# Block products in the first pass over d_ff for two more groups of tokens, and four plain blocks for the last group's second pass

## The chip, the cores and the metric

The kernel runs on one core of one Trainium2 chip. The metric is the device time of one execution in microseconds; the time before is the median of three runs, 629.42 us (628.07 to 630.46). The engines are PE (TensorE), ACT (ScalarE), DVE (VectorE), POOL (GpSimd) and SP (SyncE, whose queue issues all DMAs here); PEld is PE's weight load, which overlaps its matmuls.

## The reference, cut to what matters

An attention with two sets of keys per query, and a feed-forward layer with softplus on its result:

```python
# q, k, v: (4, 8, 768, 64), float32; block 32, window 16
k_sum = k.reshape(B, H, 24, 32, D).max(axis=3)         # one key per block of 32
v_sum = v.reshape(B, H, 24, 32, D).mean(axis=3)
scores_l = scale * q @ k^T, kept where |i - j| < 16, else -1e9
scores_s = scale * q @ k_sum^T + log(32)
a = softmax over (768 local, 24 block) scores
x = (a @ [v, v_sum]) as (3072, 512)                     # tokens x d_model
h = x @ w_in                                            # w_in: (512, 2048), float64
g = max(h, 0) + log1p(exp(-|h|))                        # softplus
out = g @ w_out                                         # w_out: (2048, 512), float64
```

## The kernel before, in words

**Tiling.** The 3072 tokens are 12 chunks of 256, taken two at a time as six groups (`groups[x]`, x = 0 to 5, 512 tokens each). d_ff is 16 columns of 128 (`f` = 0 to 15). Both weight matrices do not fit at once, so there are two passes: groups 0 to 4 do columns 0 to 7, group 5 does all 16 (the second half of the weights arrives meanwhile, `arrive`), and then groups 4 down to 0 do columns 8 to 15. This is `phases`. The sums of a first pass are kept in HBM (`partial`) and added at the end of the second; the attention result of groups 0 to 4 is kept there too (`keep`) and loaded again for the second pass (`attended`).

**Precision.** Each float32 operand of the feed-forward layer is split in two fp32r parts: a rounding (`high`) and a remainder (`low`). A product is three matmuls (`TERMS`: high x high, high x low, low x high). Weights are turned from float64 bit patterns to such parts on DVE, ACT and POOL (`weights`).

**Attention** of a group runs in four units (`attention`, two chunks x two pairs of head pairs): scores on PE, a mask on DVE, exp on ACT, a normalisation, a transpose of 32 x 32 blocks on DVE, a store to HBM (`squares`) and four loads back (`pT`), then the product with the values on PE (`values`, result `xo`). The units of group x + 1 run beside the feed-forward layer of group x.

**Hidden columns, plain** (`hidden`). In the first pass, and for both halves of group 5, a column is 4 slices of d_model x 3 terms = 12 matmuls of 128 x 128 by 512 tokens into one PSUM bank `ph`. Its operand is `whole_x`, split by `prepare_whole`, or for group 5 straight from the bank.

**Hidden columns, by block products** (`hidden_pair`). In the second pass of groups 0 to 4, two columns are made together as a 2 x 2 by 2 x 2 block product with seven block products in place of eight: the four blocks are two halves of d_model and two chunks of 256 tokens. The seven left operands are three weight blocks and four sums of weight blocks (`sums_of_weights`, buffers `s0` to `s3`, listed in `s_bufs`); the seven right operands (`operand(x, 0)` to `operand(x, 6)`) are the blocks r11, r21, r22 and differences of r11, r12, r21, r22, made by `prepare` in place, with `less` (a subtraction) and `split` (a rounding and a remainder). Each product is 2 slices x 3 terms = 6 matmuls of 256 tokens, into two PSUM banks `hx` and `hy`; a copy `p1` and seven DVE combinations put the products together.

**Buffers.** Operands lie in rings `x0` to `x2` (two buffers each) and `x3` to `x6` (one each); `whole_x` uses the same rings, `x3` to `x6` for even groups and `x1`, `x2` for odd ones. The banks `ph`, `hx`, `hy` and `xo` share one ring of two PSUM banks. `t` is a ring of two for temporaries and output blocks.

**After the hidden columns** (`feed_forward`): ACT computes softplus twice (`gh` rounded, then exact in the bank), DVE the remainder `gl`, and PE adds 12 matmuls (`po`, line 1162) per column into four PSUM banks of 128 tokens x 512.

**Order.** Every step is a task added to `Order`, with an engine (or alternatives, marked a, b, c). The list `SEQUENCE` gives the order in which all tasks are issued; each engine and SP's queue work through theirs in that order, and semaphores follow from the tiles. The list is the output of a planner that estimates times; it was written anew with the change.

Of the kernel before, what the change touches and what calls it, by code (L numbers as in the profile page):

```python
# [147 lines left out]
0 3 4 162 43 1 5 6 51 7 44 8 9 10 11 12 13 14 15 16 17 18 19 20 21 22 23 24 25 26 27 28 29 30 31 32 33 153 45 47 68  # L148
154a 158a 34 155 163a 64 46 52 156 53 55 164 2 157 165 167a 72 54 35 57 189 69 36 159 59 160a 161 49 73 48 37 86 313
61 166 56 74 171 87 190 38 39 168 75 58 40 191 88 41 60 104 62 100 76a 172a 50 152 321a 180 192 176a 77 79 66 316 65  # L150
173 174 63 67 169 42 78 108 71 175 80 170 70 177 314 315 185 194 101 109 89 312 193 110 122 123 81 324 208 198 181a
103 90b 124 107 105 343 111 82 195 84 344 182 209a 91 102 136 106 196a 112a 346 183 199 184 92 93 94 95 325 83 213
178a 197 85 342 113 125 326 372 345 96 186 210 211 114 179 351 212 138 115 116 98 117 99 97 376 126b 127 317 118 120
327 214 200a 129 128 215a 130 354 137 217 131 373 246 218 380 328 329 134 330 140 132 121 141 355 133 320 119 135 201
247 319 356 248 390 255 249 392 393 331 223a 357 187 389 334 332 318 374 322 333 391 202 204 250 256 257 188 262 203
139 258 323 216a 358 259 359 263 227 219a 377 264 251 269 270 252 205 146a 398a 271 384 360 378 265 206a 401 375 220
272 253 266 228a 335 347 350 232 353 221 254 260 402 336 273 381 361 420 229 423 421 143 276 362 363 348 230 364 419
385 403 277 349 422 283 352 338 261 222 379a 382 404 386 284 231 428 278 236 279 237 207a 280 405b 267 431 285 286 365
233 406 407 234 515 366 516 224 268 274 287 432 433 238a 368a 235 383a 290 387a 394 291 408 396 388 225 292 149a 434
239 240 520a 517 297 241 410 411 400 397 340 409 275 298 226 435a 436 242 523 299 293 395 281 399 693 542 243 294 282  # L160
412 437 524 541 546a 424 370 543 426 300 244a 438 288 341a 525 245 147a 440 289 301 429 427 441 295 339 413 439 549
430 296 425 526 567 417 369 527 303 568 569 305 570 528 550 304 529 442 697 518 415 522 309 443 416a 302 447a 371a
418a 571 445a 448 446 576a 519 551 521 530 142 533 552 306a 449 450 532 553 451 458 531 459 452 453 554 579 597 598
600 307 599 460 601 454 699 455 555 456 695 461 580 606a 465 466 581 694 467 462 534 609 711 698 714 556 310a 457 535a
558 713 544 582 144 696 468 719a 710 583a 584 463 610 559 469 611 537 612 464 705 470 548 700 557 712 547 613a 545 414
585 472 473 539 474 701 475 479 476 150a 480 481 471 722 560 148 741 145 743 614 482 572 483 477 742 486 723 740 586
587 588 574 724 487 578 702 478 484 744 577 488 489 561a 575 573 706 589 493 749a 703 494 485 538 615 495 725 496 490
707 752 590 591 595a 497 771 770 491 500 726 540a 501 616 492 602 565a 727 593 563 603 608 594 618 502 503 753 617 504
566a 604 605 619 775a 704a 607 498 499 508 505 772 620 151 728 311 337 754 778 621a 564 625 506 715 596a 729 755 623
624 626a 627 628 708 731 796 756b 629 757 797 732 630 507 636 631 716 798 948 717 637 643 709 638 644 801a 720 639 730  # L170
718 645 721 640 650 651 646 509 779 804 652 647 653 758 949 444 654 308 510a 952 733 657 734a 367 889 664 658 632 665
892 759 633 512 891 780 781 782 760 745 513 634 888 562 956 953 635 641 642 897a 783 957 747 890 762 751 805 659 648
666 761 750 748 746 738 660 950 667 784 900 806 661 763 668 736a 764a 536 919 920 785 649 671 678 672 768a 807 773 922
786 655 673 679 808a 788 809 927 787 766a 674 680 954 774 776 777 921 918 675 656 737 769a 810 662 681 960 789 511 799
901 902 803 811 800 814 682 790a 930 951 663 669 670 813 676 966 903 904b 812 802 792a 905 677 683 815 816 818 968 820
794a 739a 931 767a 821 795a 793a 819 822 906 592 965 958 969 967 893 735 684 898 686 961 899 791 823 932 933 896 895
514 934 907 824 685 974a 825 687a 831 908 909 935 826 817 832 833 690 834 977 996 827 838 978 835 839 894 910 688a 845
691 840 955 841 842 959a 828 999 997 979 846 998 995 936 911 962 1004 937 980 923 925 847 848 1007 981 1092 829 830
836 849 982 837 852 939 1091 940 1093 853 926 843 1008 1096 924 928 854 855 856 1099 963 929 938 983 912 916a 689 941
1009 622 984 964 859 860 970 975 942 944 985 861 1010 973 862 1011 844 972 850 866 914 867 987 1012 868 1116 971 863  # L180
986 873 976 1120 1117 874 1115 1100 1013 869 692 870 875 988 876 765 1014 1000 1003 913 1123 946a 989a 1101 993 1140
1016 945 851 1015 857 915a 1427 917a 1428 1561 877 1562 858 864 865 871 872 994 1102 991a 878 1017 1002 1103a 1005
1143 1001 992 947a 1104 1124 1006 881 1018 1148a 880 879 1563 1019a 990 1142 1105 1021a 1022a 1125 882a 1023a 1433
1139 1024 1141 1025 1026 1094 1027 1028 1151 1034 1029 1035 1095 1030 1041 1567 1042 883 1167 1036 1106 1107 1037 1043
1109 1038 1168 1020 1108 1048 1170 1097 1126 1127a 1044 1049 1098 1050 1051 885 1045 1110 1128 1031 1113 1111 1171
1169 886a 1118 1129 1052 1130 1152 1153 1112 1114 1131 1032 1122 1033 1055 1154 1056 1062 1057 943 1133 1119 1155 1058
1063 1039 1132 1040 1429a 1046 1176 1179 1156 887 1121 1064 1437 1059 1134 1047 1065 1157 1066 1180 1135 1181 1182
1183a 884 1137 1144 1150 1158 1160 1136 1146 1145 1149 1053 1069 1161 1159 1147 1070 1054 1060 1071 1072 1434 1138
1162 1184 1163 1073 1061 1185 1076 1165 1571 1077 1078 1166 1440 1441a 1067 1068 1079 1080 1172 1173 1186 1568a 1074
1075 1081 1085a 1187 1164 1174 1084 1083 1177 1188 1178 1175 1438 1088 1439a 1442 1189 1190 1193 1191 1194 1082 1192  # L190
1086a 1087 1195 1196 1197 1198 1204 1205 1206 1089 1199 1207 1253 1254 1208 1574 1211 1200 1212 1271 1272 1218 1219
1276 1201 1213 1273 1214 1289 1220 1221 1274 1255 1202 1215 1225 1203 1275 1277 1278 1226 1256 1257 1258 1222 1232
1262 1290 1227 1233 1291 1279a 1209 1228 1210 1259 1216 1260 1261 1308 1263a 1292 1264 1267 1346 1294 1234 1235 1229
# [40 lines left out]
def kernel(  # L234
# [639 lines left out]
    def weights(pair):  # L874
# [6 lines left out]
        for outer, which in tiles:  # L881
# [81 lines left out]
            )  # L963


    s_bufs = {}

    def sums_of_weights(f):

# [365 lines left out]
```

## Time and profile before

| | |
|---|---|
| median of three runs | 629.42 us (628.07 to 630.46) |
| the profiled execution | 630.05 us, its span 628.3 us |
| mean granted clock of TensorE | 0.983 |
| PE busy / PEld busy | 609.2 us (97%) / 508.9 us (81%) |
| DVE / ACT / POOL busy | 388.0 (62%) / 328.0 (52%) / 162.0 us (26%) |
| moved by DMA | 104.39 MB, 166 GB/s on average |
| plain hidden columns, `ph` L1045 | 672 matmuls of 512 tokens |
| block products, `hx` and `hy` L1085 | 840 matmuls of 256 tokens |
| projections, `po` L1162 | 1152 matmuls of 512 |

Rows of the profile name an engine, a line and a tile: "PE ph L1045" is the matmul of line 1045 that writes `ph`. In the chain of work that ended last, a row has the start, the length and the number of instructions merged. In a row of grouped instructions stand the count, the busy time, the mean length of one in ns, and the idle time in front of them with what ended it. In a table of stages, the columns are the stage, its length, the busy time of PE, PEld, DVE, ACT and POOL with their instructions, the granted clock, the DMA share, and GB/s.

### The profile page before, as it was taken

The numbers are of one execution on the slowest core, as the hardware profiler recorded it, in microseconds if no ns is written. First come the engines' busy times: TensorE is split into PE (matmuls) and PEld (weight loads), VectorE is DVE, ScalarE is ACT, GpSimd is POOL, SyncE is SP. The second block draws the span as 40 slices with busy tenths as digits, with TensorE's granted clock in tenths as the row PEclk, the third lists the DMA queues.
The fourth block names the chain that finished last, engine by engine and source line by source line (L and its number), as shares of the span: only waits on it lengthen the run. The fifth ranks groups of instructions, "written<-read, shape, count | busy, mean of one in ns | idle before, by whom it ended". The sixth has DMA issues, their size and how long they took to land.

```text
span 628.3 us, 12022 instructions
## 1 busy us (share of the span) xinstructions
PE 609.2 (97%) x4452; PEld 508.9 (81%) x4452; DVE 388.0 (62%) x998; ACT 328.0 (52%) x809; POOL 162.0 (26%) x145
## 2 busy tenths in 40 slices
PE   8769999999999999999999999999999999999997
PEld 7557777788888878877888888899889899898995
DVE  5887997764457454535427979764557557655442
ACT  2898895965766676456526677441323122222220
POOL 3325435132213043002003443490111403002000
PEclk9868999999999999999999999999999999999999
DMA  9998887989998887885634632103122050030301
GB/s 303 265 272 268 254 264 233 262 261 231 272 263 253 259 268 220 254 236 158 212 116 155 222 127 84 34 34 118 51 76 78 17 185 1 35 100 1 104 32 67
DMA packets 88955, 104.39 MB, mean 166 GB/s; under 512 B 27489, under 2 KB 67009, under 8 KB 88129
## 3 DMA queue, kind: packets, MB, share of 16 engines
q1 hardware_dynamic: 88896, 103.62, 54.5%
q8 instruction: 35, 0.57, 0.4%
q14 instruction: 24, 0.19, 0.1%
HBM read 73.92 MB, written 27.26 MB: 161 GB/s over the span
## 4 chain that ended last, share of the span: by engine, by line
PE 85%; DMA 8%; SPq 3%; ACT 1%; DVE 1%; issue 1%; DVEq 0%; POOL 0%; POOLq 0%; ACTq 0%
PE po L1162 40%; PE ph L1045 21%; PE hx L1085 9%; PE hy L1085 7%; PE xo L727 3%; PE sc L629 3%; DMA raw<-w_in_dram 2%; DMA k<-kT_dram 2%; DMA squares<-tb 2%; PE warm L1236 2%; DMA kf<-kT_dram 1%; DMA q<-qT_dram 1%; DMA v<-v_hp_dram 1%; SPq L708 1%; SPq L523 1%
## 5 line engine op out<-in xcount | busy, mean ns | idle before, releaser
L1162 PE MATMUL po<-w,gh 128*128 128x512 f32 x768 | 204.2, 394 | 0.0
L1162 PEld LDWEIGHTS po<-w,gh 128*128 128x128 f32 x768 | 141.4, 188 | 30.6 <-issue 0.6
L1045 PE MATMUL ph<-xw,w 128*128 128x512 f32 x672 | 163.9, 395 | 2.1 <-DVE gl L1155 2.0
L1045 PEld LDWEIGHTS ph<-xw,w 128*128 128x128 f32 x672 | 125.6, 188 | 32.5 <-DVE gl L1155 2.8
L1162 PE MATMUL po<-w,gl 128*128 128x512 f32 x384 | 116.6, 397 | 0.0
L1162 PEld LDWEIGHTS po<-w,gl 128*128 128x128 f32 x384 | 70.9, 188 | 15.9 <-issue 0.5
L650 ACT ACTIVATE sp<-sp,nm 128x120 f32<-128x120 f32 x192 | 73.1, 382 | 5.9 <-DVE nm L642 5.7
L1147 ACT ACTIVATE gh<-hx 128x512 fp32r<-128x512 f32 x20 | 12.0, 599 | 114.9 <-DVE hx L1095 114.9
L948 POOL TENSOR_TENSOR t<-t,raw 128x1024 int32<-128x1024 int32 (+1 forms) x20 | 42.4, 2122 | 98.8 <-DVE t L934 28.4
L1155 DVE TENSOR_TENSOR gl<-ph,gh 128x512 fp32r<-128x512 f32 x56 | 38.0, 684 | 40.8 <-ACT ph L1151 39.3
L1147 ACT ACTIVATE gh<-ph 128x512 fp32r<-128x512 f32 x56 | 33.5, 598 | 53.4 <-PE ph L1045 48.5
L789 POOL TENSOR_TENSOR x<-r,x 128x512 fp32r<-128x512 f32 x18 | 24.5, 1370 | 82.0 <-ACT x L782 32.2
L642 DVE CUSTOM_DVE_ANT_0 sp<-sc,added 128x120 f32<-128x120 f32 x192 | 40.8, 277 | 4.9 <-PE sc L629 3.9
L663 POOL TENSOR_TENSOR sp<-sp,ss 128x960 f32<-128x960 f32 x10 | 18.4, 1843 | 87.6 <-DVE ss L658 62.8
L650 ACT ACTIVATION_READ_ACCUMULATOR sp<-sp,nm 128x1 f32 x192 | 36.0, 187 | 0.0
L1085 PE MATMUL hx<-x,sw 128*128 128x256 f32 x240 | 35.4, 283 | 0.0
L1085 PE MATMUL hx<-x,w 128*128 128x256 f32 x240 | 35.1, 282 | 0.0
L1085 PEld LDWEIGHTS hx<-x,w 128*128 128x128 f32 x240 | 32.8, 189 | 1.9
L696 DVE STREAM_TRANSPOSE tb<-sp 128x1024 f32<-128x1024 f32 x20 | 24.8, 1242 | 15.2 <-POOL sp L663 7.9
L1085 PE MATMUL hy<-x,sw 128*128 128x256 f32 x240 | 33.2, 282 | 0.0
L1151 ACT ACTIVATE ph<-ph 128x512 f32<-128x512 f32 x56 | 32.8, 591 | 0.0
L1085 PEld LDWEIGHTS hx<-x,sw 128*128 128x128 f32 x240 | 31.7, 189 | 0.5
(108 smaller groups left out, 821.6 us busy)
## 6 DMA issues: line engine op xcount, KB each, us to landing
squares<-tb SPq DMA_DIRECT2D x20, 512.0 KB
pT<-squares SPq DMA_DIRECT2D x80, 128.0 KB
raw<-w_out_dram SPq DMA_DIRECT2D x16, 512.0 KB
kf<-kT_dram SPq DMA_DIRECT2D x16, 384.0 KB
raw<-w_in_dram SPq DMA_DIRECT2D x6, 1024.0 KB
q<-qT_dram SPq DMA_DIRECT2D x20, 256.0 KB
raw<-r SPq DMA_DIRECT2D x20, 256.0 KB
part<-ob SPq DMA_DIRECT2D x10, 512.0 KB
```

What stands on the lines that cost most here:

```text
L629: nc.tensor.matmul(unit(g * NU + h * NPAIR + i)[r * QW:(r + 1) * QW, k0:k1], lhsT=q[rows, w * QW:(w + 1) * QW], rhs=k[rows], start=True, s ...
L642: nc.vector.tensor_tensor_reduce(out=sp()[:, n], in0=unit(n), in1=added()[:, kinds.index((lows[w], lows[w + 1]))], scale=-SCALE, scalar=FL ...
L650: nc.scalar.activation(sp()[:, n], sp()[:, n], AF.Exp, bias=nm()[:, n:n + 1], scale=-1.0, accum_out=ss()[:, n:n + 1],)
L696: nc.vector.transpose(out=tb().rearrange("p k (u q) -> p u k q", q=SQ), in_=tiles.sp().rearrange("p u (k q) -> p u k q", q=SQ),)
L789: engine.tensor_tensor(to(1), a(), to(0).bitcast(F32), op=ALU.subtract)
L948: nc.gpsimd.tensor_tensor(a, a, word(0, I32), op=ALU.add)
L1045: nc.tensor.matmul(ph(), lhsT=lhs(part, cc), rhs=xw[cc][0]()[:, xw[cc][1], a], start=cc == 0 and n == 0, stop=cc == NCC - 1 and n == 2,)
L1085: nc.tensor.matmul(to()[:, half], lhsT=lhs(wa, cc), rhs=of_x(xa)[:, cc * CH:(cc + 1) * CH], start=cc == 0 and m == 0, stop=cc == NG - 1 an ...
L1147: nc.scalar.activation(gh(), all_of(), AF.Softplus)
L1151: nc.scalar.activation(all_of(), all_of(), AF.Softplus)
L1155: nc.vector.tensor_sub(out=gl(), in0=all_of(), in1=gh().bitcast(F32))
L1162: nc.tensor.matmul(po[t](), lhsT=a()[:, t * P:(t + 1) * P], rhs=w2()[:, part, i2 * DM:(i2 + 1) * DM], start=f == f0 and i == 0, stop=f == ...
```

## The change

- Groups 4 and 5 (`SEVEN = 4` and above) make columns 0 to 7 by `hidden_pair` too. For that, the sums of the first half's weights are computed after the attention of group 4 is declared, and `attend` calls `prepare` in place of `prepare_whole` for them; group 5 takes its attention result to a block `r` first.
- Group 5's columns 8 to 15 are made by a new `hidden_blocks`: each chunk of 256 tokens by itself, from operands 0, 1 and 3 and the block r12, which is split for it into a third buffer of ring `x0`.
- The six loads of the first batch's v take the buffers of rings r0 to r2 in place of ring `gh`; keys and values of later batches would go to ring `t` if sums of weights existed by then.
- `SEQUENCE` is another list (2214 tasks, 2099 before). The computation of the attention is as before.

```diff
+    SEVEN = 4
 ...
-                part = buffer([P, DM], F32, "vn0", tag="gh", bufs=NU)
+                part = buffer([P, DM], F32, "vn0", tag=f"r{i // 2}", bufs=2)
 ...
-        if x and x < NX - 1:
+        if x and (x < NX - 1 or x >= SEVEN):
             r = block(2 * i + hp // NG)
 ...
             split(r11, *operand(x, 2), NG * CH)
+            if x == NX - 1:
+                held = single[x] = buffer([P, 2, NG, CH], F32R, "x", tag="x0", bufs=2)
+                split(r12, lambda part: held()[:, part].rearrange("p g c -> p (g c)"), (held,), NG * CH)
 ...
+    def hidden_blocks(x, f):
+        w, lhs = of_w(f)
+        ph = bank([P, CT], "ph")
+        x12 = single[x]
+        blocks = {(0, 0): operand(x, 0), (0, 1): operand(x, 1), (1, 1): operand(x, 3)}
+        blocks[1, 0] = (lambda part: x12()[:, part].rearrange("p g c -> p (g c)")), (x12,)
+        def product(i):
+            for hp in range(2):
+                of_x = blocks[i, hp][0]
+                for cc in range(NG):
+                    for n, (part, a) in enumerate(TERMS):
+                        nc.tensor.matmul(
+                            ph()[:, i * CH:(i + 1) * CH], lhsT=lhs(part, hp * NG + cc),
+                            rhs=of_x(a)[:, cc * CH:(cc + 1) * CH],
+                            start=hp == cc == n == 0, stop=hp == 1 and cc == NG - 1 and n == 2,
+                        )
+        for i in range(2):
+            task = order.add(PE, 1.43, lambda i=i: product(i), ..., [ph])
 ...
     def hidden(x, f):
+        if x >= SEVEN:
+            return hidden_blocks(x, f)
 ...
-        pairs = f0 > 0
+        plain = range(HALF, NF) if x == NX - 1 else range(HALF) if x < SEVEN else ()
         for f in range(f0, f1):
 ...
+            pairs = not (f0 <= f < f1 and f in plain)
 ...
                 if x < NX - 1:
                     keep(x, n, r[n])
+                if x >= SEVEN:
+                    prepare(x, n, r)
+                elif x < NX - 1:
                     prepare_whole(x, n, r)
 ...
             sums = attend(x, sums)
+            if x == SEVEN:
+                for f in range(0, HALF, 2):
+                    sums_of_weights(f)
```

More of the change, by code (lines that the diff above doesn't have):

```diff
@@ L153 @@
[L153 to L182, printed above, removed]
@@ new lines @@
+1568 1566 1472 1575 1460a 1571 1569 1573 1574 1576 1579 1577 1469a 1578 1678a 1519 1525 1572 1526 1580 1586 1587 1581
+1588 1591 1592 1593 1820 1532 1810 1473 1683 1594 1533 1534 1474a 1600 1536a 1535 1475a 1476a 1477a 1539 1537a 1597
+1582 1540a 1601 1583 1595 1602 1598 1596 1603 1604 1605 1599 1584 1606 1607 1585 1611 1612 1589 1813 1608 1613 1616
+1619 1618 1617 1620 1622 1621 1625 1689 1623 1624 1681a 1627 1590 1629 1626 1628 1630 1631 1636 1632 1609 1610 1637
+1684 1633 1614 1638 1685a 1641 1811a 1644 1642a 1692a 1645 1816 1647 1615 1541 1643 1693a 1646 1650 1648 1652 1694
@@ L230 @@
+2136 2072 2134 2132 2140 2076 2137 2119 2139 2135 2141 2142 2147 2143 2148 2120 2144 2149 2121 2125 2152 2155 2153a
+2126 2154 2156 2158 2159 2163 2157 2161 2165 2162 2166 2164 2167 2160 2168 2172 2169 2145 2146 2173 2174 2150 2177
+2180 2178a 2183 2179 2181 2184 2182 2186 2188 2151 2073 2187 2185 2189 2170 2192 2193 2171 2190 2194 2077 2191 2175
+2204 2209 2197 2176 2198 2199 2195 2196 2203 2202 2211 2200 2210 2213 2201 2205 2212 2206 2207 2208
 """
@@ L361, in declare @@
             for i in range(NHP):
-                kf = buffer([P, S], F32, "kf", tag=f"s{i % 2}", pool=wts, bufs=1)
-                st = buffer([P, n_t, P], F32, "st", tag=f"s{2 + i % 2}", pool=wts, bufs=1)
+                if s_bufs:
+                    kf = buffer([P, S], F32, "kf", "t", T_BUFS, dynamic=True)
+                    st = buffer([P, n_t, P], F32, "st", "t", T_BUFS, dynamic=True)
+                else:
+                    kf = buffer([P, S], F32, "kf", tag=f"s{i % 2}", pool=wts, bufs=1)
+                    st = buffer([P, n_t, P], F32, "st", tag=f"s{2 + i % 2}", pool=wts, bufs=1)
                 def load_k(i=i, kf=kf):
@@ L446, in keep_first @@
                 order.add(SP, 0.4, keep, [self.first_v], [(self.v, hp)], size=12 * KiB, row=512)
-    x_bufs = {}
+    x_bufs, s_bufs = {}, {}
     def x_of(x):
@@ L963, in weights @@
             )
-    s_bufs = {}
     def sums_of_weights(f):
-        order.group = f"s{f}"
+        order.group = f"s{f}" if f >= HALF else f"z{f}"
         a = buffer([P, 2, 2, CH], F32, "ws", "t", T_BUFS, dynamic=True)
@@ L975, in sums_of_weights @@
         begun = [order.writer[w, part] for w in held for part in range(2)]
-        if f == HALF - 2:
-            begun.append(products[-1])
         for k, w in enumerate(held):
@@ L1034, in of_w @@
         return w, lambda part, cc: w()[:, part, (cc * n + i) * P:(cc * n + i + 1) * P]
+    single = {}
+    def hidden_blocks(x, f):
[15 more added lines that the diff above has]
+        for i in range(2):
+            task = order.add(
+                PE, 1.43, lambda i=i: product(i),
+                [(*blocks[i, hp][1], part) for part in range(2) for hp in range(2)] + [(w, part) for part in range(2)],
+                [ph],
+            )
+            if not i:
+                first_after(task)
+        return [ph]
     def hidden(x, f):
+        if x >= SEVEN:
+            return hidden_blocks(x, f)
         w, lhs = of_w(f)
@@ L1140, in feed_forward, with all_of @@
             gl = buffer([P, CT], F32R, "gl", bufs=4)
-            def all_of(h=h):
+            def all_of(h=h, pairs=pairs):
                 return h().rearrange("p n c -> p (n c)") if pairs else h()
```

130 lines of the change are left out of this document (78 added, 52 removed).

## The prediction

> **What bounds the kernel now.** I read the page first, then a table of stages, the chain that ended last, and the waits.
>
> ```profile
> span 628.3 us, 12022 instructions
> PE 609.2 (97%) x4452; PEld 508.9 (81%) x4452; DVE 388.0 (62%) x998; ACT 328.0 (52%) x809; POOL 162.0 (26%) x145
> ```
> ```profile
> 0.00:51.90 51.90, 41.05 (x572) 32.85 (x572) 37.77 (x137) 35.67 (x123) 20.25 (x36) 0.80 1.00 285
> 51.90:110.00 58.10, 55.40 (x452) 42.75 (x449) 50.20 (x144) 47.89 (x121) 23.86 (x16) 1.00 0.84 249
> 110.00:322.00 212.00, 210.98 (x1699) 169.24 (x1699) 112.23 (x385) 134.73 (x389) 44.77 (x46) 1.00 0.81 237
> 322.00:412.00 90.00, 90.00 (x438) 74.24 (x439) 69.84 (x92) 55.74 (x77) 36.57 (x20) 1.00 0.35 120
> 412.00:628.30 216.30, 211.75 (x1303) 189.86 (x1301) 118.01 (x242) 53.98 (x102) 36.53 (x29) 1.00 0.19 65
> ```
>
> The stage rows give length, then busy time of PE, PEld, DVE, ACT and POOL, then granted clock, DMA share and GB/s. There are two regimes. Up to 51.9 us the DMA engines are full (share 1.00, 285 GB/s) and PE has holes; the granted clock is 0.80 there. From 110 us to the end PE is busy for 512.7 of 518.3 us, and 4.5 us of the rest are the last additions and stores, from 623.79 us on. A busy PE is modelled, so I check it with the chain, where a piece's length is the time really taken:
>
> ```profile
> 383.95 5.55 PE ph L1045 x24
> ...
> 594.40 1.43 PE hx L1085 x12
> 595.83 1.43 PE hy L1085 x12
> 597.25 1.43 PE hx L1085 x12
> 598.68 0.72 PE hy L1085 x6
> 599.40 4.61 PE po L1162 x20
> ...
> 623.79 0.69 DVE ob L1192
> ```
> ```profile
> PE xo L727 <- ACT pT L687: 4.2, 2, 2.4
> PE ph L1045 <- DVE gl L1155: 2.0, 2, 1.2
> ```
>
> The pieces follow each other without a gap, and the longest waits of PE (last two rows: total, times, longest) lie in the start. So after the start the time is the sum of what PE must issue, and a change of PE's work moves the end one for one, as long as the other engines keep up.
>
> **The change, part by part.**
>
> *Eight pairs of first-pass columns as block products.* Groups 4 and 5 each have 8 columns of d_ff in the first pass, 4 pairs each. A plain pair is 2 x 12 matmuls of 512 columns: the row at 383.95 has 24 of them in 5.55 us. A block pair is 7 products x 2 x 3 = 42 matmuls of 256 columns: the four rows from 594.40 have 42, and the next piece starts at 599.40, so 5.00 us. Saved: 8 x 0.55 = 4.4 us.
>
> *The last group's second pass from four plain blocks.* 24 matmuls of 256 columns (24/42 x 5.00 = 2.86 us) take the place of 12 of 512 (2.775 us): 8 x 0.08 = 0.66 us lost. PE's net is **-3.7 us**. Projections, scores and values are unchanged.
>
> The Trainium skill ("TensorE: Matmul & The Clock Gate", section "Wait — 56ns, not 53.3ns?") gives a back-to-back matmul as N / 2.4 GHz plus some 2.5 ns, an estimate of 216 and 109 ns; this trace has 5.55/24 = 231 and 5.00/42 = 119 ns. By the page the net would be -4.5 us; the rows decide, so -3.7 us.
>
> *What the block pairs ask of the other engines.* These rows price it:
>
> ```profile
> L1095 DVE TENSOR_TENSOR hx<-hx,u 128x256 f32<-128x256 f32 x20 | 8.6, 431 | 7.3 <-PE hx L1085 6.8
> L1104 ACT COPY p<-hx 128x256 f32<-128x256 f32 x8 | 3.0, 374 | 23.4 <-PE hx L1085 23.4
> L782 ACT CAST x<-r 128x512 fp32r<-128x512 f32 x21 | 12.8, 616 | 20.3 <-PE ph L1045 4.9 <-PE hy L1085 4.9 <-DMA r<-raw 4.8
> L789 DVE TENSOR_TENSOR x<-r,x x17: 676/682/1770, 267.4 to 567.7; 128x512 fp32r<-128x512 f32 x17
> L789 POOL TENSOR_TENSOR x<-r,x x18: 1285/1296/1832, 294.1 to 570.4; 128x512 fp32r<-128x512 f32 x18
> L797 DVE TENSOR_TENSOR r<-r 128x512 f32<-128x512 f32 x10 | 6.9, 687 | 1.4 <-POOL x L789 1.2
> L739 ACT COPY r<-xo 128x512 f32<-128x512 f32 x8 | 4.6, 580 | 7.5 <-PE xo L727 7.5
> L985 POOL TENSOR_TENSOR ws<-w 128x512 f32<-128x512 f32 x4 | 7.5, 1900 | 0.0
> L993 POOL TENSOR_TENSOR ws<-ws 128x256 f32<-128x256 f32 x1 | 0.7, 736 | 0.0
> L1016 POOL TENSOR_TENSOR sw<-ws,sw 128x1024 fp32r<-128x1024 f32 x2 | 4.8, 2394 | 1.2 <-ACT sw L1009 1.2
> 216.00:270.00 54.00, 54.00 (x452) 43.37 (x451) 28.16 (x107) 36.57 (x112) 13.36 (x14) 1.00 0.85 252
> 270.00:322.00 52.00, 50.98 (x358) 40.61 (x358) 22.93 (x69) 25.46 (x67) 6.34 (x5) 1.00 0.60 181
> 322.00:366.00 44.00, 44.00 (x218) 35.90 (x219) 31.62 (x45) 25.84 (x38) 13.94 (x9) 1.00 0.55 194
> 366.00:412.00 46.00, 46.00 (x221) 38.34 (x220) 38.22 (x48) 29.89 (x40) 22.64 (x11) 1.00 0.15 50
> ```
>
> Each pair adds 7 combinations on DVE (7 x 0.43 = 3.0 us) and a copy on ACT (0.37): 24 and 3 us over 8 pairs. Operands: each group now needs 7 splits of 512 columns (the last group one more, x12): a rounding (ACT 0.62) and a remainder (DVE 0.68 or POOL 1.30 at the median), and 4 subtractions (DVE 0.69), in place of 8 roundings and remainders of half the width; the last group also copies four banks (ACT 0.58). That is some 10 us more per group. The sums of the first half's weights, four times, are two or more POOL sums of 1.9 us, four small ones of 0.74, a rounding on ACT and a remainder (POOL 2.39). None of it is on PE. It lies beside group 4's first pass (270 to 322 us) and group 5's (322 to 366), where DVE is at 22.93 of 52 and 31.62 of 44 us. I went through the new order and added the row times of what each engine is given between the first product of a stage and that of the next: DVE has 41 us in the 53 us of PE's group 4 first pass, 36 in 42 in group 5's first pass, 31 in 40 in its second: 78, 86, 77%. The kernel before runs the 90 us from 322 with DVE at 69.84 (78%) and PE without a hole; 366 to 412 is at 83%. So throughput suffices; what can be lost is latency, at places where PE needs an operand just made. Two such places: group 3 to 4 (operands 1 and 2 lie in buffers that group 3's last plain product still reads) and 4 to 5 (operands 3 to 6, and x12, wait for group 4's last pair). In both the order leaves projections for PE between: 4.6 us per 20 (row at 599.40) against a copy, a subtraction, a rounding and a remainder, 0.6 + 0.69 + 0.62 + 1.30 = 3.2 us. Bounds: 0 when the cover holds, as between second-pass groups now, and 1.5 us at each place where it doesn't. I take +0.7 us in all. The one new wait, the rounding of x12 for the buffer of group 4's operand 0, has group 4's last softplus behind it on ACT; that softplus needs the sixth product of the pair, the rounding only the first, so it costs nothing.
>
> *Attention.* No unit is added or removed. Where `x >= SEVEN`, group 5 takes its bank into a block first. The values of a unit need a bank of the same ring of two that a pair takes whole.
>
> *The start, in a new order.* The six loads of the first v get six blocks of the r rings instead of four of gh, so this wait of the queue goes:
>
> ```profile
> SPq L423 <- PE vt L428: 1.8, 2, 1.0
> ```
> ```profile
> 104.66 3.66 DMA v<-v_hp_dram
> ```
>
> With the DMA engines full, what is late next is the bytes themselves. Task numbers below group 4 are the same in both lists, so I added the sizes that SP issues up to the last transfer that a step needs. Values of group 1: first unit 17.58 MB before, 18.68 after; second 21.61 and 22.13; third 25.64 in both; fourth 28.23 and 27.84. PE's last wait is the one before that fourth unit (the transfer at 104.66). At 249 GB/s, 0.39 MB is 1.6 us earlier; 1.1 MB in front of the first unit is up to 4.4 us later, if nothing fills PE. The first product of group 0 now stands in front of the last first-group transposes, which fills a hole. I take -0.5 us, nearest the fourth unit's row because that is where PE waits last, with -4 (the holes of the first 51.9 us: 10.9 us, of which a third might be filled) and +4.4 as ends. The wait of 1.8 us is in it.
>
> *Queues.* No transfer is added or dropped. The weights of the second half still land over those of the first once group 5 has passed them. The sums of the first half take the buffers where the last batch's keys and values were reduced, so they wait for attention of group 4, not the reverse; the branch for those keys in ring t is not reached, since no sum exists then. Cost nothing; if a sum is late, group 4's second product waits behind it on PE (bound: one sum, some 2 x 1.9 + 4 x 0.74 POOL and 2.4 us, 9 us, once).
>
> **Sum.** -3.7 (PE) +0.7 (latency) -0.5 (start) = -3.5 us. The profiled execution took 630.05 us (span 628.3), which would become 626.5; against the median of the runs, 629.42, it is **625.9 us**.
>
> **Rivals.**
>
> 1. *Latency eats the saving* (same). Eight pairs each losing 0.25 us plus 1.5 us at one handover: 3.5 us back, 629.4. For: DVE at 86% in group 5's first pass. Against: second-pass pairs lose nothing with the same seven combinations. A mechanism in the rows: the DVE remainder L789 is 0.68 at the median and 1.77 at most, and more POOL work lies beside DVE now. The Trainium skill ("GPSIMD Engine Reference", opening table, SBUF interfaces) says that GpSimd shares its SBUF interfaces with VectorE and contends with two-input instructions; that spread agrees.
>
> 2. *Attention late in group 4's first pass* (slower). The last unit takes this long now:
>
> ```profile
> 298.62 0.98 PE sc L629 x32
> ```
> ```profile
> 309.64 0.34 SPq L704 DMA_DIRECT2D squares<-tb  x1
> 321.87 1.15 PE L727 MATMUL xo<-pT,v 120*64 120x64 f32 x32
> ```
>
>    From scores to values 23.3 us, with DVE at 44%. The new order puts 23.0 us of PE work between the same two. If the mask, transpose and copy each queue behind a pair's combinations, a unit comes 2.5 us late, and PE, whose order is fixed, stops. Four units: +10 - 3.7 = +6.3, 635.7 us. It decides from (3.7 + 3.1)/4 = 1.7 us a unit. Against: the store starts 11 us after the scores, and its data had landed before PE came.
>
> 3. *The start goes better*: the holes fill by 3 to 4 us, 622.5. Against: the DMA share of 1.00.
>
> 4. *The start goes worse*: 1.1 MB in front of the first unit of group 1 is waited for in full: 629.42 - 3.7 + 0.7 + 4.4 = 630.8 (same).
>
> 5. *The change does not do what it says* would need 256-column matmuls to cost over 5.55/42 = 132 ns in the first pass; the second pass has them at 119. Under 1 in 50, inside rival 1.
>
> **How the numbers follow.** Forecast, 624 to 628: 0.50 (of it 0.38 below the bound). Rival 1: 0.20. Rival 2: 0.12. Rival 3: 0.12. Rival 4: 0.06. A change of under 0.5% (3.1 us) is what this measurement can hardly tell from none. Faster is below 626.3: 0.38 + 0.12 = 0.50; slower above 632.6: 0.12; same 0.38. The range 621.5 to 631.5 holds all but rival 2 and half of the fringes; the forecast's own is 624 to 628.
>
> **What would show it.** Right: 288 ph matmuls of 512 columns fewer, and 192 of 256 for group 5's second pass; hx and hy from 840 to 1176; PE without a wait from 110 us on, DVE near 80% between 270 and 400 us, the last attention unit on time. Wrong: PE waits for pT or for an x operand after 200 us; group 1 starting later than 110 us; a matmul of hx in the first pass longer than 119 ns.

## The result, and the profile after

The changed kernel takes 634.42 us (median of 4 runs, 633.86 to 636.03), the kernel before 629.41 us beside it (4 runs): ratio 1.0085, 95% interval [1.0058, 1.0112]. It is slower by some 5 us where 3.5 us less were forecast, and above the forecast range of 621.5 to 631.5 us. The profiled execution took 634.32 us; its page begins so:

```profile
span 632.5 us, 12633 instructions
PE 609.3 (96%) x4692; PEld 517.8 (82%) x4692; DVE 416.7 (66%) x1075; ACT 345.9 (55%) x842; POOL 191.1 (30%) x173
```

The table of stages of the changed kernel (length, busy time of PE, PEld, DVE, ACT and POOL, granted clock, DMA share, GB/s):

```profile
0.00:51.90 51.90, 40.70 (x541) 32.33 (x542) 32.61 (x125) 35.78 (x127) 19.47 (x35) 0.84 0.95 268
51.90:66.00 14.10, 10.90 (x96) 8.14 (x95) 13.16 (x34) 13.51 (x35) 3.85 (x3) 0.88 0.91 288
66.00:110.00 44.00, 41.35 (x338) 31.98 (x336) 42.24 (x104) 37.52 (x100) 17.80 (x10) 1.00 0.82 224
110.00:322.00 212.00, 211.34 (x1837) 172.29 (x1826) 135.56 (x443) 140.99 (x393) 70.72 (x73) 1.00 0.82 240
322.00:412.00 90.00, 89.97 (x575) 81.21 (x575) 72.87 (x125) 62.96 (x84) 38.56 (x24) 1.00 0.34 121
412.00:632.50 220.50, 215.02 (x1323) 191.88 (x1321) 120.27 (x248) 55.18 (x105) 40.73 (x30) 1.00 0.20 67
```

And the two stages of the kernel before that the prediction gave as one:

```profile
51.90:66.00 14.10, 13.24 (x58) 9.93 (x54) 12.19 (x31) 13.66 (x32) 6.88 (x5) 1.00 0.84 234
66.00:110.00 44.00, 42.15 (x395) 32.82 (x395) 38.00 (x114) 34.23 (x91) 16.98 (x12) 1.00 0.84 253
```

Between 51.9 and 66 us PE is 2.3 us less busy, at a granted clock of 0.88 in place of 1.00. (Over the whole execution the mean granted clock is 0.983 in both traces: in total the changed kernel is at half the clock no longer than the kernel before.) A busy time says too little here, since a matmul that waits or runs at half the clock counts as busy. So I laid each kernel's matmuls beside their order and gave each its length in an undisturbed stretch (0.231 us for 512 columns of ph, 0.230 of po, 0.119 for 256 columns, 0.031 a score, 0.034 a value). A time T minus the lengths of what PE has issued by T is the time that PE has lost by then (the warm-up is not counted as work). By these lengths all work together is 583.8 us before and 580.05 after: the block products do give 3.75 us. What PE had lost, in us:

| by the time (us) | 50 | 65 | 115 | 200 | 320 | 400 | 440 | end |
|---|---|---|---|---|---|---|---|---|
| before | 27.5 | 29.7 | 33.8 | 35.3 | 38.9 | 39.2 | 39.3 | 39.5 |
| changed | 28.0 | 34.0 | 38.9 | 42.2 | 44.7 | 45.7 | 48.0 | 48.3 |
| difference | 0.5 | 4.3 | 5.1 | 6.9 | 5.8 | 6.5 | 8.7 | 8.8 |

The difference of 8.8 less 3.75 is the 5 us of the medians (the two spans differ by 4.2: behind the last matmul 4.1 us are left, 4.9 before). 3.8 us of it come between 50 and 65 us, in group 0, and 2.2 between 400 and 440. Another 2.6 come between 65 and 200; of these 1.5 are listed waits of PE (3.2 us, most of them for `gl`, against 1.7), and the rest was not followed. From 200 to 320 us, which holds group 4's first pass, the changed kernel gains 1.1: the kernel before waits 1.0 us there, at 274.70, for ACT's `gh`.

**50 to 66 us.** PE in the kernel before, then in the changed one (start, length; idle time ahead and its releaser in brackets):

```profile
51.94 6.23 PE L1045 MATMUL ph<-xw,w 128*128 128x512 f32 x24
58.91 3.07 PE L1045 MATMUL ph<-xw,w 128*128 128x512 f32 x12 [0.74 <-DVE gl L1155]
```
```profile
54.08 1.15 PE L737 MATMUL xo<-pT,first 120*64 120x64 f32 x32
57.01 0.50 PE L1086 MATMUL ph<-xw,w 128*128 128x512 f32 x1 [1.78 <-ACT xw L767]
58.13 4.29 PE L1086 MATMUL ph<-xw,w 128*128 128x512 f32 x11 [0.62 <-DVE xw L771]
63.21 1.05 PE L639 MATMUL sc<-k,q 64*64 64x120 f32 x32 [0.80 <-ACT k L523]
```

Before, 24 products of columns 0 and 1 stand behind the last values of group 0, and the second operand is made under the first of them. In the new order 12 of them stand ahead of the values, so after the values nothing covers the 2.4 us in which ACT and DVE make the operand. The 11 matmuls after this hole take 4.29 us where 12 took 3.07, some 1.5 us more; with the 2.3 us that PE is less busy this makes the 3.8. Their clock:

```profile
58.00:61.40 3.40, 3.27 (x8) 2.60 (x9) 3.37 (x7) 3.38 (x15) 0.83 (x1) 0.50 1.03 326
```

So a hole of 2.4 us was followed by 3.4 us at half the clock. The Trainium skill ("TensorE: Matmul & The Clock Gate", section "Part 1: The HAM clock gate") has two clocks only, half and full, judged in windows of about 3.4 us; this row agrees in both numbers, though the hole was shorter than such a window.

ACT is what is late. Its rows in the changed kernel, then before:

```profile
55.55 1.15 ACT L935 ACTIVATE t<-raw 128x1024 f32<-128x1024 f32 x1
...
60.52 1.28 ACT L1189 ACT_TABLE_LOAD   x1
61.81 0.60 ACT L1189 ACTIVATE gh<-ph 128x512 fp32r<-128x512 f32 x1
...
63.06 2.23 ACT L953 ACTIVATE raw<-raw 128x1024 int32<-128x1024 uint32 x2
65.20 2.38 ACT L676 ACTIVATE sp<-sp,ss 128x120 f32<-128x120 f32 x8
67.49 0.57 ACT L1189 ACTIVATE gh<-ph 128x512 fp32r<-128x512 f32 x1
```
```profile
55.75 1.28 ACT L1147 ACT_TABLE_LOAD   x1
57.04 0.60 ACT L1147 ACTIVATE gh<-ph 128x512 fp32r<-128x512 f32 x1
...
59.61 0.57 ACT L1147 ACTIVATE gh<-ph 128x512 fp32r<-128x512 f32 x1
...
60.68 1.28 ACT L922 ACT_TABLE_LOAD   x1
...
63.16 1.28 ACT L1147 ACT_TABLE_LOAD   x1
...
67.08 1.28 ACT L922 ACT_TABLE_LOAD   x1
```

The softplus of column 1 (the second `gh` row) starts at 67.49 us, 17.2 us after the first product (50.30); before it was 7.7 us after it (59.61, 51.94). Ahead of it stand conversions of weights (L935, L953) and a normalisation (L676) that the order before did later or on another engine. Added up from the traces, ACT has worked 66.3 us by the start of that step in the changed kernel and 56.0 in the kernel before, 10.2 us more: 6.1 are two more normalisations, 3.1 conversions of weights. DVE has 57.3 against 55.7, 1.6 us more.

**425 us.** One wait of PE in the second pass, and behind it DVE and POOL of the changed kernel:

```profile
423.16 2.39 POOL L1025 TENSOR_TENSOR sw<-ws,sw 128x1024 fp32r<-128x1024 f32 x1 [6.29 <-DVE sw L1018]
...
425.59 0.69 DVE L1238 COPY ob<-po 128x512 f32<-128x512 f32 x1 [1.90 <-POOL sw L1025]
...
427.13 0.98 PE L1126 MATMUL hx<-x,sw 128*128 128x256 f32 x6 [1.73 <-DVE u L1136]
```

An output copy takes a buffer of ring `t` that a sum of weights still holds until POOL's remainder is made. DVE waits 1.90 us at the copy, the combinations of the next pair stand behind it, and PE waits 1.73 us for them. What such a hole costs is not always the same. The stretch behind it in the changed kernel, then in the profiled execution of run 11, which has the same wait of 1.73 us:

```profile
428.00:431.40 3.40, 3.40 (x19) 2.90 (x19) 2.15 (x5) 2.18 (x4) 0.00 (x0) 1.00 0.91 314
```
```profile
428.00:431.40 3.40, 3.40 (x15) 2.98 (x14) 2.16 (x6) 1.52 (x3) 0.00 (x0) 0.58 0.88 302
```

The granted clock stays at 1.00 in the one and is 0.58 in the other, where PE loses some 1.3 us more between 400 and 440 us.

**What was forecast of the blocks holds.** In the changed kernel, from the chain of waits, the groups of PE, and the stages of the prediction:

```profile
386.39 5.72 PE ph L1060 x48
```
```profile
L1086 PE MATMUL ph<-xw,w 128*128 128x512 f32 x384 | 97.2, 402 | 4.5 <-DVE gl L1197 2.1
...
L1060 PE MATMUL ph<-x,w 128*128 128x256 f32 x192 | 23.8, 282 | 0.0
```
```profile
270.00:322.00 52.00, 52.00 (x466) 45.40 (x465) 37.25 (x97) 33.14 (x83) 14.27 (x13) 1.00 0.58 178
322.00:366.00 44.00, 43.97 (x270) 38.99 (x270) 37.46 (x75) 27.74 (x40) 19.67 (x16) 1.00 0.55 193
366.00:412.00 46.00, 46.00 (x306) 42.22 (x305) 35.42 (x51) 35.22 (x45) 18.89 (x8) 1.00 0.14 51
```

288 plain matmuls fewer (672 to 384), 192 of 256 columns for group 5, 5.72/48 = 0.119 us each; DVE at 72, 85 and 77% of the three stages, and PE without a hole.

### The profile page after: what moved, and what is told of

Its sections match the earlier page's. It is cut to its first block, busy times and chain, and to the rows that moved or that the text cites. A ratio compares the mean times of both kernels' runs of the same rounds, so it can differ in the third digit from the quotient of the medians.

```text
span 632.5 us, 12633 instructions
## 1 busy us (share of the span) xinstructions
PE 609.3 (96%) x4692; PEld 517.8 (82%) x4692; DVE 416.7 (66%) x1075; ACT 345.9 (55%) x842; POOL 191.1 (30%) x173
## 3 DMA queue, kind: packets, MB, share of 16 engines
q1 hardware_dynamic: 88896, 103.62, 54.4%
## 4 chain that ended last, share of the span: by engine, by line
PE 81%; DVE 7%; DMA 5%; ACT 3%; SPq 2%; issue 1%; POOL 1%; ACTq 0%; DVEq 0%
PE po L1204 39%; PE hx L1126 12%; PE ph L1086 11%; PE hy L1126 9%; PE ph L1060 4%; PE xo L737 3%; PE sc L639 2%; DMA first<-v 1%; DMA kf<-kT_dram 1%; DMA raw<-w_in_dram 1%; ACT sp L676 1%; DMA k<-kT_dram 1%; DVE st L390 1%; DVE r L783 1%; DVE w L972 1%
## 5 line engine op out<-in xcount | busy, mean ns | idle before, releaser
L1086 PE MATMUL ph<-xw,w 128*128 128x512 f32 x384 | 97.2, 402 | 4.5 <-DVE gl L1197 2.1
L1086 PEld LDWEIGHTS ph<-xw,w 128*128 128x128 f32 x384 | 72.7, 192 | 22.3 <-DVE gl L1197 2.5
L799 POOL TENSOR_TENSOR x<-r,x 128x512 fp32r<-128x512 f32 x30 | 40.6, 1356 | 133.6 <-ACT x L792 77.0
L1126 PE MATMUL hx<-x,sw 128*128 128x256 f32 x336 | 49.2, 282 | 1.7 <-DVE u L1136 1.7
L1126 PE MATMUL hx<-x,w 128*128 128x256 f32 x336 | 49.3, 282 | 0.0
L1126 PEld LDWEIGHTS hx<-x,w 128*128 128x128 f32 x336 | 45.8, 189 | 3.7 <-DVE u L1136 0.3
L1126 PEld LDWEIGHTS hx<-x,sw 128*128 128x128 f32 x336 | 44.1, 188 | 2.7 <-DVE u L1136 2.2
L1126 PE MATMUL hy<-x,sw 128*128 128x256 f32 x336 | 45.6, 281 | 0.0
L1126 PEld LDWEIGHTS hy<-x,sw 128*128 128x128 f32 x336 | 42.7, 188 | 0.5
L1189 ACT ACTIVATE gh<-ph 128x512 fp32r<-128x512 f32 x40 | 23.9, 598 | 33.8 <-PE ph L1086 23.7
L792 ACT CAST x<-r 128x512 fp32r<-128x512 f32 x31 | 18.5, 617 | 26.2 <-POOL r L808 9.0
```

The costliest lines, as they stand in the source:

```text
L792: copy(out=to(0), in_=a())
L799: engine.tensor_tensor(to(1), a(), to(0).bitcast(F32), op=ALU.subtract)
L1086: nc.tensor.matmul(ph(), lhsT=lhs(part, cc), rhs=xw[cc][0]()[:, xw[cc][1], a], start=cc == 0 and n == 0, stop=cc == NCC - 1 and n == 2,)
L1126: nc.tensor.matmul(to()[:, half], lhsT=lhs(wa, cc), rhs=of_x(xa)[:, cc * CH:(cc + 1) * CH], start=cc == 0 and m == 0, stop=cc == NG - 1 an ...
L1189: nc.scalar.activation(gh(), all_of(), AF.Softplus)
```

## The experiments

All ratios are to the kernel before, run in turn on the same chip (its median was 630.3 to 631.3 us there), with 95% intervals. Where two orders are put together, "first n" means the first n steps of a list, followed by the other list's steps that are not among them.

**1. Start of before in the changed kernel** (first 658 steps, up to group 2; the rings stay).
```diff
-SEQUENCE = changed
+SEQUENCE = before[:658] + [s for s in changed if s not in before[:658]]
```


> The changed kernel with the order of the kernel before for every task up to the first product of group 2 (the first 658 entries of the old list), and the new order for all the rest. Theory A, the new order of the start costs the time: PE loses about 6.5 us less up to group 2, so 634.4 - 6.5 = 628 us, a little faster than before. Theory B, the block products of groups 4 and 5 cost it (DVE and ACT fuller, PE waits behind them): the start hardly matters, 633 to 635 us. Theory C, half of each: 631 us.

632.21 us, 1.0024 [0.9996, 1.0052]. PE had lost 28.8 us at 65 us (34.0 in the changed kernel), but 40.1 at 200 (42.2): the gain of the start is seen, 5.2 us, and 2.1 of it are left behind the seam, which lies at 167 us, the first product of group 2. By its ratio the run comes out at theory C, half of each; the later runs, with other seams and the copy moved, do not bear that out.

**2. Start of the changed kernel in the kernel before** (first 663 steps, with the rings).
```diff
-SEQUENCE = before
+SEQUENCE = changed[:663] + [s for s in before if s not in changed[:663]]
-part = buffer([P, DM], F32, "vn0", tag="gh", bufs=NU)
+part = buffer([P, DM], F32, "vn0", tag=f"r{i // 2}", bufs=2)
```


> The kernel before (no new block products) with the new order for every task up to the first product of group 2, with the first v loads in the r rings as the new order needs, and the old order for all the rest. Theory A: the loss comes with the order alone, 629.4 + 6.5 = 636 us. Theory B: 629 to 630 us. Theory C: 632 to 633 us.

639.85 us, 1.0124 [1.0088, 1.0160]: without any block product in a first pass, the new start with its rings costs as much as the whole change does, or more. PE had lost 35.9 us at 65 us.

**3. The rings of the first v alone**, in the kernel before.
```diff
-part = buffer([P, DM], F32, "vn0", tag="gh", bufs=NU)
+part = buffer([P, DM], F32, "vn0", tag=f"r{i // 2}", bufs=2)
```


> The kernel before in its own order; only the six loads of the first v lie in the r rings in place of the gh ring. Theory A in its narrow form (the order, not the buffers): 629 to 630 us, with the two waits of the queue on the v sums (1.8 us) gone and nothing gained, since the DMA engines are full there. The rival, that the buffers make the start worse or better: 2 us or more off 629.4.

632.87 us, 1.0036 [1.0012, 1.0060]. An edit that I had costed as a small gain loses some 2 us here.

**4. The output copy of 425 us behind the next pair's combinations**, in the changed kernel.
```diff
-1582 1540a 1601 1583 1595 1602 1598 1596 1603
+1582 1601 1583 1595 1602 1598 1596 1540a 1603
```


> The changed kernel with one entry of the list moved: the last DVE copy of group 5's output block (it waits on DVE for the t buffer of the last weight sum, with the combinations of the next pair behind it) comes three DVE steps later. If that wait is what stops PE for 1.9 us at 425 us: 632.5 us. If PE only waits elsewhere instead: 634.4 us.

634.23 us, 1.0054 [1.0030, 1.0077]. The stall is gone (47.9 lost at 400 us, 48.1 at 440); the profiled execution had lost more earlier. The intervals of this and of the changed kernel overlap, so its price was measured again (run 10).

**5 and 6. Single moves on ACT and POOL in the changed start.**
```diff
-398a 250 203 401 331 334 251 218 252 204 232 332 357 358b 420 333 231 257 258 215a
+398a 257 258 250 259 203 401 331 334 251 218 252 204 232 332 357 358b 420 333 231 215a
```


> The changed kernel with one thing moved: ACT's two softplus steps of column 1 of group 0 stand in front of the two weight roundings and the normalisation that the new order has ahead of them (and DVE's remainder gl of that column directly behind). Nothing else. Theory A1 (the start is slow because ACT makes weight parts and normalises before the first columns' softplus; gh of column 1 comes at 67.5 us where it came at 59.6): about 3 us of the 5 that PE loses between 55 and 66 us come back, 631.5 us, ratio to before 1.003 to 1.005. Rival A2 (it is not that order on ACT but what else the new start has earlier, DVE and DMA included): within 1 us of the changed kernel, 634, ratio 1.0085.

```diff
-328b
+328
-358b
+358
-435b
+435
```


> The changed kernel with the three normalisations that the new order gives ACT in the first 75 us (8 small instructions each, 2.4 us) on POOL, where the order before had them. Theory A1 in its other part: ACT is 2.4 us freer ahead of the late softplus, so 1.5 to 2.4 us come back: 632 to 633, ratio 1.005 to 1.006. Rival: POOL takes 5 us or more for one of them, its transposed store and the values of group 1 come later, and the time stays at 634 or rises.

634.40 us, 1.0078 [1.0051, 1.0106], and 637.41 us, 1.0110 [1.0088, 1.0132]. Neither brings anything back that the runs resolve. With the softplus first, the scores wait 1.92 us for a copy of k that now stands behind it on ACT; its profiled execution, the fastest of six, took 632.32 us. In it, behind the hole ahead of the operand (2.7 us here, 1.77 and 0.97), PE's 11 matmuls are these:

```profile
57.00 2.82 PE L1086 MATMUL ph<-xw,w 128*128 128x512 f32 x11 [0.97 <-DVE xw L771]
```

They take 2.82 us where the changed kernel took 4.29: this hole was not followed by half the clock. With POOL normalising, PE had lost 36.6 us at 100 and 40.9 at 115; from 105.4 to 108.8 us the granted clock is 0.50.

**7 and 8. Before's order up to group 3, and the copy moved**, with the rings and without.
```diff
-SEQUENCE = changed
+SEQUENCE = before[:838] + [s for s in changed if s not in before[:838]]    # group 4's steps by their new numbers; and 1540a as in 4
```


> The changed kernel with the order of before for the first 838 steps (up to group 3's first product) and the output copy of 425 us moved behind the next pair's combinations; the first v still in rings r. Theory (block products save 3.7 us as summed, the start's new order costs 5 to 6.5, the stall at 425 us 1.9, the r rings some 2): 3.7 below before plus 2.3 for the rings and some 1 at the seam of the lists: 629 to 630.5 where before has 630, ratio 0.998 to 1.001. Rival B (the block products themselves cost time after 200 us): 633 or more, ratio 1.005 or more.

> As the run before it in this call, but with the first v in ring gh as in the kernel before. If the r rings cost the 2.3 us that their run alone showed: 626.5 to 628, ratio 0.994 to 0.997, faster than both kernels. If the rings' cost was of that order alone: the same as the run before it within 1 us. Rival B as there: 633 or more.

633.72 us, 1.0060 [1.0040, 1.0079], and 631.86 us, 1.0018 [1.0001, 1.0035]. Both missed what the theory said. Of the run without the rings, PE had lost 36.5 us at 200 us (35.3 in the kernel before) and 44.6 at 260: the seam of the lists costs some 7 us. 3.8 of them are waits of PE (2.9 for ACT's `sp`, 0.9 for k); from 219.2 to 226.0 us the granted clock is 0.50. The chain of waits names what is late, loads that are issued just in time for work which the first list had already done:

```profile
206.94 5.34 DMA v<-v_hp_dram
...
216.78 4.04 DMA k<-kT_dram
```

From 260 us to the end this run loses 1.5 us, the kernel before 2.9. So the blocks were not the cause, and the seam had to be put where the two lists agree. By the nearest places of both lists, 17 steps stand in only one of them at this seam and 10 at that of run 1; at the 427th step of before (some 105 us) it is 5.

**9 and 10. Seam at the 427th step, without the rings**, with the copy moved, and without.
```diff
-SEQUENCE = changed
+SEQUENCE = before[:427] + [s for s in changed if s not in before[:427]]    # 9: and 1540a as in 4
```


> The changed kernel with the order of before for its first 427 steps (up to about 105 us, where the two lists have nearly the same steps behind them), the first v in ring gh as before, and the output copy of 425 us moved behind the next pair's combinations. Theory (the start's new order, the rings and the copy are the whole loss; the block products give their 3.7 us): before has lost 33.8 us of PE time at 115 us, the changed kernel loses 9.4 from there to the end, less 2.2 for the copy, so 41.0 in all beside 580.05 us of work, 2.4 us under the kernel before: 628, ratio 0.994 to 0.998. Rival (the changed order from 110 us on costs what the blocks bring, whatever the start): 630 or more, ratio 1.000 or more.

> The same without the moved copy. If the stall at 425 us costs what the trace shows, 1.7 to 2.2 us more than the run before it in this call: ratio 0.998 to 1.001. Rival: the 1.7 us are made up later, as the second pass has idle time on DVE: no difference.

626.95 us, 0.9939 [0.9922, 0.9956], and 629.13 us, 0.9974 [0.9957, 0.9991]. Run 9 came as the theory had it; run 10 lies just under its range, with the expected difference between the two. Run 9 is faster than both kernels, with all of the change's block products. Its stages, as above:

```profile
51.90:66.00 14.10, 13.49 (x77) 10.79 (x74) 11.28 (x33) 12.55 (x29) 7.28 (x4) 0.91 0.85 252
66.00:110.00 44.00, 42.95 (x399) 33.24 (x398) 41.83 (x121) 35.09 (x94) 15.44 (x11) 1.00 0.84 250
110.00:322.00 212.00, 210.72 (x1805) 172.16 (x1805) 133.63 (x426) 141.38 (x393) 70.62 (x72) 1.00 0.81 235
```

PE had lost 31.0 us at 65 us, 34.2 at 115, 41.1 at the end, against 34.0, 38.9 and 48.3 in the changed kernel. The copy costs 0.35% or 2.2 us by the two runs, 2.1 by their traces (41.2 lost at 400 us, 43.3 at 440, without the move).

**11 and 12. Two more moves in the changed start**: the first products behind the values; two conversions behind the parts of x, with the softplus first.
```diff
-127 328b 246 129 320
+127 328b 129 320
-212 186 255 228a 120
+212 186 228a 120
-391 131 121
+391 131 246 255 121
```


> The changed kernel with the first halves of columns 0 and 1 of group 0 (4 pieces of PE work of 1.39 us are in those two columns) behind the last values of group 0, as in the order before, in place of ahead of them. They then cover the 2.4 us in which PE waits for ACT's and DVE's parts of x at 55 to 58 us, and the hole at 50 to 53 us that they fill now opens again. Theory C (the hole is only moved): the same as the changed kernel within 1 us, 634, ratio 1.007 to 1.009. Rival (losing the cover is the loss): 2 to 2.5 us less, ratio 1.004.

```diff
-186 255 228a 120
+186 255 120
-134 200a 355 132 135
+134 355 132 228a 200a 135    # and 257, 258, 259 as in run 5
```


> The changed kernel with four things moved on ACT: the two weight conversions that stand ahead of the parts of x at 55 us go behind them, and the softplus of column 1 goes ahead of the two others and of the normalisation, as in the run softplus_first. Theory A3 (ACT is late at both places, and each alone only hands the wait on to the other): 2 to 3 us come back, ratio 1.003 to 1.005. Rival (ACT has more to do in front of 66 us than in the order before whatever its sequence, and the weights come late instead): within 1 us of the changed kernel, ratio 1.007 to 1.009.

636.20 us, 1.0081 [1.0063, 1.0100], and 637.33 us, 1.0091 [1.0069, 1.0113]: the hole is only moved, and no single piece of the new start, put back, mends it. Run 11 had lost 0.5 us more than the changed kernel by 320 us; in both profiled executions the wait at 425 us was followed by half the clock, which adds some 1.3 us that is not of the start.

**13. Run 9 with the rings.** The edit is that of run 3, in run 9.

> As start1_late_gh (0.9939 of the kernel before), with the first v in the r rings, as the changed kernel has it. Theory (the rings cost some 2.5 us, as two pairs of runs showed: +0.36% alone, and 0.42% between start3_late and start3_late_gh): ratio 0.997 to 0.999. Rival (the rings cost only where the order around them is another): 0.993 to 0.996.

628.04 us, 0.9950 [0.9929, 0.9972]. The intervals of 9 and 13 overlap: in this order the rings cost 0.1%, not resolved from nothing, against 0.4% in runs 3 and 7. The theory missed and its rival held. No run takes the rings out of the changed order.

**14 and 15. Each half of the start by itself.**
```diff
-SEQUENCE = before[:427] + [s for s in changed if s not in before[:427]]
+SEQUENCE = before[:203] + [s for s in changed if s not in before[:203]]    # 14, no rings
+SEQUENCE = changed[:202] + [s for s in before[:427] if s not in changed[:202]] + [the rest of changed]    # 15, rings
```


> Order of before for the first 203 steps (up to about 50 us, where group 0's first product stands), then the changed order; first v in ring gh, the copy late, as in start1_late_gh. Theory D (the loss is in the order from 50 us on: by the row times ACT has 4.5 us and DVE 4.3 us more ahead of column 1's softplus): 4 to 6 us above start1_late_gh, ratio 1.000 to 1.004. Rival E (it is in the order of the first 50 us, its loads included): within 1 us of it, 0.993 to 0.996.

> The complement: the changed order for the first 202 steps (some 50 us), the order of before from there to its 427th step, then the changed order; first v in the r rings, the copy late; to be read against start1_late. Theory D: within 1 us of start1_late. Rival E: 4 to 6 us above it. Two orders meet at 50 us, a seam that may cost 1 to 3 us by itself in both runs.

630.89 us, 0.9995 [0.9976, 1.0014], and 638.25 us, 1.0098 [1.0069, 1.0128]. (The 4.5 us of ACT and 4.3 of DVE in the first expectation are 10.2 and 1.6 when added up from the traces.) With the new order from 50 us on, run 14 lies 0.56% above run 9 (3.5 us), and PE loses 10.1 us from 50 to 115 where run 9 loses 6.4. Run 15 lies 1.5% above run 13 and contradicts theory D as put, but its seam at 50 us, where 18 steps stand in only one of the lists, cannot be told from the order of the first 50 us: by the halves alone the split stays open.

**16 to 18. Pieces of the new start in the good order of run 9.**
```diff
-125 326 372
+125 326 227 372                                      # 16 and 17: the load of 1 MB
-130 354 ... 249 392 ... 204 250 256 257
+130 228a 354 ... 249 229 230 392 ... 204 232 250 256 358b 257    # 16: conversion steps and normalisation
-256 257
+256 358b 257                                         # 18: the normalisation on ACT alone
```


> start1_late_gh with six steps brought forward to where the changed order has them: the load and two ACT steps of the third weight slab's conversion (1.1 us each), its two DVE steps (clamp and shift), and the normalisation of one unit of group 1 on ACT (2.4 us) in place of POOL, ahead of column 1's softplus. Theory D in its mechanism (work that is not due yet stands ahead of the softplus and the parts of x): PE loses 2 to 4 us between 55 and 66 us, ratio 0.997 to 1.000. Rival (ACT and DVE have room for it there): within 1 us of start1_late_gh, 0.993 to 0.996.

> start1_late_gh with only the load of the third weight slab's first 1 MB brought forward, to where the changed order and w3_early have it (41.6 us in place of 63.5 in the trace of w3_early); none of its conversion steps is moved. Theory F (w3_early lost its 5.8 us in the queue: while the DMA engines are full, 1 MB not yet due is 3.7 us at 285 GB/s ahead of the keys, which came 1.7 us late at 51.6 us): 2 to 5 us above start1_late_gh, ratio 0.997 to 1.002. Theory D (ACT and DVE): within 1 us of it, 0.993 to 0.996.

> start1_late_gh with only the normalisation of one unit of group 1 (eight instructions, 2.4 us) on ACT ahead of column 1's softplus, as the changed order has it, in place of POOL after it. Theory D: the softplus comes some 2 us later, and PE, which has the columns 2 and 3 to do meanwhile, loses 1 to 2.4 us: ratio 0.996 to 0.998. Theory F: within 1 us of start1_late_gh, 0.993 to 0.996.

633.31 us, 1.0031 [1.0006, 1.0055]; 629.01 us, 0.9974 [0.9956, 0.9992]; 628.00 us, 0.9969 [0.9946, 0.9992]. Six steps brought forward cost 0.92%, some 5.8 us, more than was expected of them. The load alone costs 0.35% and the normalisation alone 0.30%, though the latter's interval overlaps that of run 9 and the former's begins where it ends. Theory F in run 17 and theory D in run 18 each came within its range. The wait of PE with the load early and a table of the stretch behind it, then ACT's softplus and the waits of PE with the normalisation on ACT:

```profile
52.59 1.08 PE L639 MATMUL sc<-k,q 64*64 64x120 f32 x16 [2.97 <-DMA k<-kT_dram]
```
```profile
52.00:58.00 6.00, 5.42 (x54) 4.52 (x55) 5.65 (x24) 2.39 (x12) 1.17 (x1) 0.50 1.03 349
```
```profile
61.47 0.60 ACT L1189 ACTIVATE gh<-ph 128x512 fp32r<-128x512 f32 x1
...
63.32 3.05 PE L1086 MATMUL ph<-xw,w 128*128 128x512 f32 x12 [1.07 <-DVE gl L1197]
...
71.33 1.15 PE L737 MATMUL xo<-pT,v 120*64 120x64 f32 x32 [2.16 <-DVE gl L1197]
```

With 1 MB ahead of them that is not due, PE waits 3 us for the keys, for which run 9 does not wait here, and the 6 us after the hole run at a clock of 0.50. That clock is not all the hole's doing, since run 9 is at half the clock up to 54.4 us without it; in run 17 it lasts until 58.9. Run 9:

```profile
47.60:54.30 6.70, 6.68 (x73) 4.94 (x73) 4.85 (x21) 4.64 (x15) 5.77 (x4) 0.50 1.04 355
```

In run 18, the softplus of column 1 comes 10.0 us after the first product (61.47, the product at 51.5), 7.7 in run 9, and PE waits for `gl` behind it, 4.3 us in all against 1.6.

## Why the prediction was wrong, point by point

- **PE's net of -3.7 us: right.** The work is 3.75 us less, each matmul at its forecast length, and run 9 is 0.61% faster, some 3.8 us (2.8 to 4.9 by its interval). That the change does not do what it says (rival 5) is out.
- **Other engines, groups 4 and 5: right.** DVE stands at 72, 85 and 77% where I had added up 78, 86 and 77; attention is on time; between 200 and 420 us PE has no wait at all. So rival 2 fell, and rival 1 with it: no pair of the first pass and neither of the two handovers in the sum loses anything.
- **Latency +0.7 us: nothing was lost at the two places I named, which is the lower of their bounds, and a third place was missed.** The copy at 425 us costs 2.2 us. I had followed the sums of the first half through ring `t`, but not the sums of the second half, whose steps the new list moves against the output copies that share the ring.
- **The start, -0.5 us: the step that failed.** Measured: with the copy's 0.35% taken off, the changed kernel is 1.1% slower than run 9, some 7 us, of which the rings are 0.7 by run 13's median and up to some 2.5 by runs 3 and 7. I priced the start by the bytes that SP issues and by one hole that the first product fills. The place of that price was misread, too: the transfer at 104.66 is a piece of the chain, not a wait. In the list of PE's waits of the kernel before stand, between 66 and 110 us, 1.24 us for `gl` and 0.54 for k; the values that follow the transfer start without idle time:

```profile
107.96 1.44 PE L727 MATMUL xo<-pT,v 120*64 120x64 f32 x32
```

At 1.44 us for 32 where the other groups' values take 1.15, an earlier transfer had some 0.3 us to give there, not 1.6. Neither ACT's nor DVE's order was gone through in the start, as it was for groups 4 and 5; the same sum would have shown ACT with 10.2 us more ahead of column 1's softplus. The hole was filled with work that had been the cover of the next operand.
- **Rival 4 named the right place** with the wrong mechanism: its bytes ahead of group 1's first unit bounded the loss at 4.4 us. That unit's values did not wait. The bound held only for the queue, yet I took it for the whole start, so the range ended at 631.5.
- **"Wrong if group 1 starts later than 110 us"** was the sign that came: 115.3 us (110.1 in the kernel before, 110.6 in run 9). The stated wait for an x operand also came, but at 57 us, not after 200.
- **The rings**, "in it" as a gain of 1.8 us, cost 0.36% [0.12, 0.60] alone. That the wait of the queue which they take away only kept loads back which were not due is a reading that no run tests.

Shown: that the start's order with its rings, and the copy, turn a gain of 0.6% into a loss of 0.85% (runs 2, 9, 10 and 13). Shown in part: bringing a load and ACT's work forward costs each some 0.3% (17, 18, hardly clear of run 9), and together with the conversions 0.9% (16). Open: how the changed start's own loss divides between loads, rings, ACT and DVE, as no single move mended it, and how much of it is the clock, whose stretches at half speed lie elsewhere in every trace.

## What to carry to other kernels

When a whole order is written anew with an edit, cost every engine's list in every stage, above all in the stage that is already short of slack; the place of the edit may be the only one that behaves as planned. Work used to fill a hole is no longer there to cover the next wait, and a step brought forward on a full queue or engine delays what was due. A piece of the chain that ended last is not yet a wait: read the idle time in front of it before pricing it. To join two orders, put the seam where both have nearly the same steps behind them: the same edit cost 7 us at one seam and under 1 us at another.

## What the runs showed of the hardware that I had not expected

- A hole of 2 to 3 us on PE can cost more than itself, and need not. 2.4 us idle were followed by 3.4 us at a granted clock of 0.50 in the changed kernel; 2.7 us in run 5 were not. The same 1.7 us at 425 us were followed by it in run 11 and not in the changed kernel. In the clock records of these traces every stretch at 0.50 from 10 us to the last matmul lasts 3.4 us or a multiple of it; what decides whether a hole is followed by one, no run here shows.
- Fewer table loads on ACT did not help. Between 53 and 69 us the changed kernel has one, at 60.52; the kernel before has four of 1.28 us there (its rows stand in the fence on ACT), and still its softplus is earlier. The Trainium skill ("ScalarE: Activation LUTs", section "What ACT_TABLE_LOAD costs") adds a drain and comes to 2.66 us a switch; here the load starts at 55.75 and the softplus at 57.04, 1.3 us in all, and the measurement decides.
